# The rotation's sums of the second batch moved from VectorE to accumulating transfers that GpSimd issues

## The chip, the cores and the metric

The kernel runs on one core of a Trainium2 chip. The metric is device time in microseconds (us) of one execution; lower is better.

## The reference

Four batches of eight heads, 576 positions, head size 64. Queries and keys are rotated by position, attention is a plain softmax, and its output feeds a gated layer of 512 to 1536 to 512 features:

```python
def rotate(x):
    x1, x2 = (x[..., :half], x[..., half:])
    return np.concatenate([x1 * cos - x2 * sin, x1 * sin + x2 * cos], axis=-1)
q_rot, k_rot = (rotate(q), rotate(k))
scores = scale * np.matmul(q_rot, k_rot.transpose(0, 1, 3, 2))
attn = softmax(scores)                     # maximum subtracted, sum + 1e-9
x = np.matmul(attn, v)                     # heads side by side: 2304 x 512
out = (1 / (1 + np.exp(-(x @ w_gate))) * (x @ w_val)) @ w_out
```

The inputs are float32, and large enough (q, k and w_gate are scaled up) that the kernel carries most operands as two float16 terms. w_gate, w_val and w_out come in as 64-bit words that the kernel decodes on the chip.

## The kernel before, in words

**Tiling.** Heads go in pairs, two heads of 64 rows to the 128 partitions, so a batch has four pairs p = 0 to 3 (`NP`). For each pair the rotation needs `x`, which holds key and query side by side (128 x 2 x 576 float32, 576 KB), and `y`, the same with the halves of each head swapped (the tile `sw`, also 576 KB). With m = 0 for the keys and m = 1 for the queries, three operations each give `x = x*cos + y*sin`: the product of `x` (L416), the product of `y` (L418) and the sum (L420).

**Where the tiles lie.** Batches 0 and 1 keep `x` in `qk0[p]`, which is a piece of the tile `stk`, and TensorE takes their scores from it in float32 (L470). Batches 2 and 3 use two other buffers, `qk`, and go on into float16 terms (L482). The buffers of `sw` are two for all batches, in turn: pair p = 2 of batch 1 gets the one that p = 0 had, p = 3 the one of p = 1, and the first two pairs of batch 2 follow in the same way. A reload of `sw` (L412) therefore waits for the last operation that reads the old contents, which is the sum.

**Engines.** The rotation is done by VectorE for batches 0 and 1 and by GpSimd for batches 2 and 3. All transfers are issued by SyncE, in one queue and in one order: loads of `x` (L411) and `sw` (L412), of v (L379), of the words of w_out (L348), a copy between partition halves (L534, shown as p<-p), and the transposes of the attention weights (L537, shown as pt<-p), on which the product of weights and v waits (L547). A transfer whose semaphore isn't there yet holds all that is behind it in that queue.

**Order.** All operations are given to a planner (`Plan`) with a rank, a cost and the tiles that they read and write; it plays them through once and fixes the order of every engine and of the transfer queue. Costs are in us; `land=(a, b)` makes a task a transfer that holds one common bus for a and is complete b later. VectorE and GpSimd share a `port` in this model. Only the order comes out of it, with the waits that the data need.

**Stages.** The first 200 us decode w_gate, w_val and w_out on VectorE and ScalarE (L295, L298, L302, L354) while batch 0's attention runs. The last third of w_out's decoding, the end of batch 0's attention and the rotation of batch 1 meet between 160 and 230 us of the span. Then comes the hidden layer of batch 0's second half (L598), the first long run of matmuls, whose scale needs a maximum over partitions (`allmax`, L252, L254 on VectorE, L257).

Of the kernel before, what the change touches and what calls it, by code (L numbers as in the profile page):

```python
# [16 lines left out]
ALU = mybir.AluOpType  # L17
# [17 lines left out]
class Plan:  # L35
# [27 lines left out]
    def order(self):  # L63
        N = len(self.tasks)
        succ = [[] for _ in range(N)]
        left = [len(p) for p in self.preds]
        for n, p in enumerate(self.preds):
            for m in p:
                succ[m].append(n)
        free, wait, ready, done = {}, {}, {}, [None] * N  # L70

        def offer(n):
            for e, _ in self.tasks[n][0]:
                t = 0.0
                for m in self.preds[n]:
                    e0, end, land = done[m]
                    t = max(t, end if e0 == e and not land else end + land + self.HOP)
                heapq.heappush(wait.setdefault(e, []), (t, self.tasks[n][1], n))
                ready.setdefault(e, [])
                free.setdefault(e, 0.0)  # L80

        for n in range(N):
            if not left[n]:
                offer(n)
        starts, bus, port = [], 0.0, 0.0
        while len(starts) < N:
            best = None
            for e in free:
                w, r = wait[e], ready[e]
                while w and done[w[0][2]]:  # L90
                    heapq.heappop(w)
                while r and done[r[0][1]]:
                    heapq.heappop(r)
                if r or w:
                    t = free[e] if r else max(free[e], w[0][0])
                    if best is None or t < best[0]:
                        best = (t, e)
            t, e = best
            w, r = wait[e], ready[e]
            while w and w[0][0] <= t:  # L100
                _, rank, n = heapq.heappop(w)
                if not done[n]:
                    heapq.heappush(r, (rank, n))

            held = e in ("DVE", "POOL") and port > t + 0.2
            fit = [x for x in r if not held or (e == "DVE" and not self.tasks[x[1]][4])]
            if fit:
                x = min(fit)
                r.remove(x)
                heapq.heapify(r)  # L110
            else:
                x = heapq.heappop(r)
            n = x[1]
            where, rank, fn, land, locks = self.tasks[n]
            cost = dict(where)[e]
            if e == "POOL" or (e == "DVE" and locks):
                t = max(t, port)
                port = t + cost
            if land:

                bus = max(bus, t + cost) + land[0]
                done[n] = (e, t + cost, bus + land[1] - t - cost)
            else:
                done[n] = (e, t + cost, 0.0)
            free[e] = t + cost
            starts.append((t, n, e))
            for m in succ[n]:
                left[m] -= 1
                if not left[m]:
                    offer(m)  # L130
        self.done = done
        return sorted(starts)
# [7 lines left out]
def c_dve(n, psum=False, two=False):  # L140
    return 0.07 + n / 960 + (0.08 if psum else 0) + (0.1 if two else 0)


def c_act(n):
    return 0.24 + n * 0.0009


def c_pool(n, two=False):
    return 0.16 + n * (0.0025 if two else 0.0011)
# [7 lines left out]
def rope_attention_then_sigmoid_glu(ctx: ExitStack, tc: tile.TileContext, qk, v, w_in, w_out, tables, out):  # L157
    nc = tc.nc
    V, A, G, T, Y = nc.vector, nc.scalar, nc.gpsimd, nc.tensor, nc.sync
# [48 lines left out]
    P = Plan()  # L208
    turn = {}

    def ring(name, n):
        k = turn[name] = (turn.get(name, -1) + 1) % n
        return k

    def op(e, us, rank, reads, writes, fn, port=False):
        P.add(((e, us),), rank, reads, writes, lambda _: fn(eng.get(e)), port=port)
# [4 lines left out]
    def either(places, rank, reads, writes, fn, port=True):  # L221
        P.add(tuple(places), rank, reads, writes, lambda e: fn(eng[e]), port=port)

    def dma(rank, reads, writes, kb, fn, also=()):
        P.add((("SP", 0.45),), rank, reads, writes, lambda _: fn(), land=(kb / 280, 1.6), also=also)
# [7 lines left out]
    def tiny(rank, reads, writes, fn, us=0.2):  # L233
        op("DVE", us, rank, reads, writes, lambda E: fn())
# [26 lines left out]
    def allsum(rank, src, n, where, reads):  # L261

        ps, Z = where
        mm(0.4, rank, reads + ["zero"], [Z], lambda: T.matmul(ps[:, 0:n], lhsT=ones, rhs=src, start=True, stop=True))
        return ps[:, 0:n]
# [3 lines left out]
    def m_place():  # L269
        m = ring("m", 3)  # L270
        return m_ps[m], ("m", m)
# [127 lines left out]
    def keys_queries(b, p, rank):  # L399

        z = ring("sw", 2)
        Z = [("sw", z, m) for m in range(2)]
        if b < NW:
            x, X = qk0[p], [("stk", n) for n in range(8 * p, 8 * p + 8)]
            X = [X[0:4], X[4:8]]
        else:
            r = ring("qk", 2)
            x, X = qkr[r], [[("qk", r, m)] for m in range(2)]
        y = sw[z]
        early = -8.5 if b == p == 0 else rank - 0.1  # L410
        dma(early, [], X[0] + X[1], 576, lambda: Y.dma_start(out=x, in_=qk[b, p, 0]))  # L411
        dma(early, [], Z, 576, lambda: Y.dma_start(out=y, in_=qk[b, p, 1]))  # L412
        gate = ["tab"] + ([("ws", 8 + p)] if b == 1 else [])
        places = [("POOL", c_pool(S, two=True))] if b > 1 else [("DVE", c_dve(S, two=True))]
        for m in range(2):
            either(places, rank, gate, X[m], lambda E, m=m: E.tensor_tensor(  # L416
                out=x[:, m], in0=x[:, m], in1=tab[:, 0], op=ALU.mult))
            either(places, rank, gate, [Z[m]], lambda E, m=m: E.tensor_tensor(  # L418
                out=y[:, m], in0=y[:, m], in1=tab[:, 1], op=ALU.mult))
            either(places, rank, [Z[m]], X[m], lambda E, m=m: E.tensor_tensor(  # L420
                out=x[:, m], in0=x[:, m], in1=y[:, m], op=ALU.add))
        if b < NW:
            slots[b, p] = p, None, -1.0 / D ** 0.5
            return
        X = X[0] + X[1]
        t, k = ring("stk", 3), ring("q_m", 4)
        M = ("q_m", k)
        e16 = y.rearrange("p m c -> p (m c)").bitcast(F16).rearrange("p (n c) -> p n c", n=4)
        for m in range(2):
            op("ACT", c_act(S) + 0.2, rank, [X[m]], ["sink", M], lambda E, m=m: A.activation(  # L430
                sink, x[:, m], AF.Abs, accum_out=q_m[:, k, m:m + 1]))
        top = allsum(rank, q_m[:, k], 2, m_place(), [M])
        Q = ("q_s", k)
        place = ("m", turn["m"])
        pow2(rank, top, q_s[:, k], q_i[:, k], 14, [place], [Q])
        n = 4 * (b - NW) + p
        se = q_e[:, n:n + 1]
        tiny(rank, [Q], [("q_e", n)], lambda: V.scalar_tensor_tensor(
            out=se, in0=q_i[:, k, 0:1], scalar=-1.0 / D ** 0.5, in1=q_i[:, k, 1:2], op0=ALU.mult, op1=ALU.mult))
        for m, hi, lo in ((0, 1, 2), (1, 0, 3)):  # L440
            op("ACT", c_act(S), rank, [X[m], Q], Z, lambda E, m=m, hi=hi: scaled(A, e16[:, hi], x[:, m], q_s[:, k, m:m + 1]))
            op2(c_dve(S, two=True), rank, [X[m], Q], Z, lambda E, m=m, hi=hi, lo=lo: rest(
                e16[:, lo], x[:, m], q_s[:, k, m:m + 1], e16[:, hi]))
        W = [("stk", n) for n in range(12 * t, 12 * t + 12)]
        for h in range(2):
            U = W[6 * h:6 * h + 6]
            hs = slice(64 * h, 64 * h + 64)
            dst = stk[:, t, h]
            dma(rank, Z, U[0:2], 216, lambda hs=hs, dst=dst: Y.dma_start(
                out=dst[0:64], in_=e16[hs, 0:3]), U)  # L450
            dma(rank, Z, U[2:3], 72, lambda hs=hs, dst=dst: Y.dma_start(
                out=dst[64:128, 0], in_=e16[hs, 3]), U)
            dma(rank, Z, U[3:4], 72, lambda hs=hs, dst=dst: Y.dma_start(
                out=dst[64:128, 1], in_=e16[hs, 2]), U)
            dma(rank, Z, U[4:6], 72, lambda hs=hs, dst=dst: Y.dma_start(
                out=dst[64:128, 2], in_=e16[hs, 1]), U)
        slots[b, p] = t, se, se
# [307 lines left out]
```

## Time and profile before

| | us |
|---|---|
| three runs, median | 740.73 |
| three runs, lowest and highest | 736.84, 741.0 |
| the profiled execution's own time | 738.06 |
| its span, first to last instruction | 736.2 |
| VectorE busy | 525.1 (71%) |
| TensorE busy | 632.9 (86%) |
| GpSimd busy | 74.9 (10%) |

Busy shares are means over the whole span. Positions in the span are in us from its first instruction. In the views, PE is TensorE, DVE VectorE, ACT ScalarE, POOL GpSimd and SP SyncE; an L with a number is the line of the kernel that issued the instruction, where helpers such as L281 (the second float16 term) stand for all that call them. "Idle before" is the time in which the engine had nothing to do, with what ended it.

### The profile page before, as it was taken

The numbers are of one execution on the slowest core, as the hardware profiler recorded it, in microseconds if no ns is written. First come the engines' busy times: TensorE is split into PE (matmuls) and PEld (weight loads), VectorE is DVE, ScalarE is ACT, GpSimd is POOL, SyncE is SP. The second block draws the span as 40 slices with busy tenths as digits, with TensorE's granted clock in tenths as the row PEclk, the third lists the DMA queues.
The fourth block names the chain that finished last, engine by engine and source line by source line (L and its number), as shares of the span: only waits on it lengthen the run. The fifth ranks groups of instructions, "written<-read, shape, count | busy, mean of one in ns | idle before, by whom it ended". The sixth has DMA issues, their size and how long they took to land.

```text
span 736.2 us, 12433 instructions
## 1 busy us (share of the span) xinstructions
PE 632.9 (86%) x4642; PEld 414.9 (56%) x4642; DVE 525.1 (71%) x1194; ACT 461.7 (63%) x940; POOL 74.9 (10%) x54
## 2 busy tenths in 40 slices
PE   2366885773199999999999899999999999999997
PEld 1134563451066644677556665587567756866753
DVE  6998899989978963787589987669968655321310
ACT  3767899876557983776666877667567655322320
POOL 0400000000033000014313022130500000000000
PEclk9999797896589999999999999999999999999999
DMA  9965744747924283387775596755774516000001
GB/s 365 316 153 133 233 154 151 195 120 203 246 83 129 52 189 93 94 187 163 160 186 134 108 202 179 165 125 119 178 152 100 131 37 151 1 1 29 1 7 37
DMA packets 187484, 100.55 MB, mean 137 GB/s; under 512 B 171040, under 2 KB 176288, under 8 KB 185376
## 3 DMA queue, kind: packets, MB, share of 16 engines
q1 hardware_dynamic: 187424, 99.77, 53.4%
q8 instruction: 36, 0.59, 0.3%
q14 instruction: 24, 0.20, 0.1%
HBM read 43.12 MB, written 4.72 MB: 65 GB/s over the span
## 4 chain that ended last, share of the span: by engine, by line
PE 69%; DVE 21%; DMA 5%; issue 3%; ACT 2%; SPq 0%; DVEq 0%; ACTq 0%
PE m L598 31%; PE m L632 19%; PE pv L547 8%; PE s L470 5%; PE s L482 4%; DVE p L281 4%; DMA pt<-p 4%; DVE p L505 3%; DVE wo L298 2%; DVE wo L302 2%; DVE w L281 1%; DVE stk L420 1%; DVE gt L281 1%; DVE sw L418 1%; DMA sw<-in_qk_dram 1%
## 5 line engine op out<-in xcount | busy, mean ns | idle before, releaser
L598 PE MATMUL m<-xt,w 128*128 128x320 f16 (+1 forms) x2304 | 302.2, 290 | 7.7 <-DVE th L608 3.5
L598 PEld LDWEIGHTS <-w 128*128 128x128 f16 x2304 | 224.6, 99 | 78.3 <-issue 14.6
L632 PE MATMUL m<-wo,gt 128*128 128x512 f16 x648 | 145.5, 379 | 1.6 <-DVE th L608 1.6
L510 ACT ACTIVATE p<-p,st 128x576 f32<-128x576 f32 x144 | 110.5, 768 | 55.5 <-DVE p L505 47.9
L281 DVE SCALAR_TENSOR_TENSOR p<-p,st,p 128x576 f16<-128x576 f32 x144 | 120.8, 868 | 21.0 <-ACT p L275 20.3
L470 PE MATMUL s<-stk 64*128 64x288 f32 (+1 forms) x320 | 70.8, 514 | 51.6 <-DVE p L505 37.2
L275 ACT ACTIVATE p<-p,st 128x576 f16<-128x576 f32 x144 | 104.4, 765 | 15.6 <-DMA pt<-p 6.4
L632 PEld LDWEIGHTS <-gt 128*128 128x128 f16 x648 | 62.4, 98 | 75.0 <-issue 5.8
L547 PE MATMUL pv<-pt,v 128*64 128x256 f16 (+3 forms) x960 | 77.2, 311 | 21.4 <-DMA pt<-p 21.4
L608 DVE SCALAR_TENSOR_TENSOR th<-th,m 128x256 f32<-128x256 f32 (+1 forms) x96 | 42.9, 450 | 68.0 <-PE m L598 65.3
L275 ACT ACTIVATE gt<-th,c_s 128x256 f16<-128x256 f32 (+1 forms) x96 | 50.3, 529 | 52.6 <-DVE th L608 51.9
L547 PEld LDWEIGHTS <-v 128*64 128x64 f16 (+1 forms) x960 | 54.6, 118 | 44.1 <-issue 30.0
L470 PEld LDWEIGHTS s<-stk 64*128 64x128 f32 (+1 forms) x320 | 35.6, 211 | 76.3 <-DVE p L505 46.8
L604 ACT ACTIVATE th<-m,gsc 128x256 f32<-128x256 f32 (+1 forms) x96 | 47.5, 494 | 41.1 <-PE m L598 40.9
L281 DVE SCALAR_TENSOR_TENSOR gt<-th,c_s,gt 128x256 f16<-128x256 f32 (+1 forms) x96 | 51.6, 542 | 18.5 <-ACT gt L275 18.3
L505 DVE TENSOR_SCALAR_CACHE_REDUCE p<-s 128x576 f32<-128x576 f32 x72 | 53.4, 750 | 15.1 <-PE s L470 14.6
L505 DVE TENSOR_SCALAR_CACHE_REDUCE p<-s,q_e 128x576 f32<-128x576 f32 x72 | 57.0, 811 | 9.8 <-PE s L482 9.3
L418 POOL TENSOR_TENSOR sw<-sw,tab 128x576 f32<-128x576 f32 x16 | 24.1, 1504 | 253.4 <-DMA sw<-in_qk_dram 222.9
L482 PE MATMUL s<-stk 128*128 128x288 f16 (+1 forms) x320 | 44.4, 287 | 3.1 <-DVE p L505 3.0
L416 POOL TENSOR_TENSOR qk<-qk,tab 128x576 f32<-128x576 f32 x16 | 25.3, 1607 | 201.7 <-DMA qk<-in_qk_dram 179.1
L482 PEld LDWEIGHTS <-stk 128*128 128x128 f16 (+1 forms) x320 | 27.5, 100 | 16.7 <-issue 8.2
L275 ACT ACTIVATE o<-m,o_s 128x512 f32<-128x512 f32 x16 | 10.9, 684 | 37.2 <-PE m L632 37.0
(94 smaller groups left out, 506.9 us busy)
## 6 DMA issues: line engine op xcount, KB each, us to landing
wo<-in_w_dram SPq DMA_DIRECT2D x12, 1024.0 KB, 5.6
sw<-in_qk_dram SPq DMA_DIRECT2D x16, 576.0 KB, 5.0
xt<-in_wo_dram SPq DMA_DIRECT2D x12, 512.0 KB, 4.7
stk<-in_qk_dram SPq DMA_DIRECT2D x8, 576.0 KB, 4.6
xt<-in_v_dram SPq DMA_DIRECT2D x4, 1152.0 KB, 7.1
qk<-in_qk_dram SPq DMA_DIRECT2D x8, 576.0 KB, 5.8
out_dram<-o SPq DMA_DIRECT2D x16, 256.0 KB, 2.0
stk<-sw SPq DMA_DIRECT2D x16, 216.0 KB, 3.5
```

Of the source, the lines that this page charges most:

```text
L275: A.activation(o, src, AF.Copy, scale=scale)
L281: V.scalar_tensor_tensor(out=o, in0=src, scalar=scale, in1=hi, op0=ALU.mult, op1=ALU.subtract)
L418: either(places, rank, gate, [Z[m]], lambda E, m=m: E.tensor_tensor(out=y[:, m], in0=y[:, m], in1=tab[:, 1], op=ALU.mult))
L470: T.matmul(s_ps[to[e]][hs if width == 64 else slice(0, 128), c, 0:288], lhsT=qT[hs, rows:rows + width], rhs=kT[hs, c * 288:c * 288 + 288], ...
L482: T.matmul(o[:, c, 0:288], lhsT=q[:, rows:rows + width], rhs=kk[:, c * 288:c * 288 + 288], start=(m == 0), stop=(m == 1))
L505: lambda E, h=h, c=c: V.tensor_scalar(out=p32[prs[c]].rearrange("p (c n) -> p c n", c=2), in0=s_ps[h][:, :, 0:288], scalar1=down, scalar2= ...
L510: lambda E, c=c: A.activation(p32[prs[c]], p32[prs[c]], AF.Exp, bias=st[:, k, 0, c:c + 1], scale=-1.0, accum_out=st[:, k, 1, c:c + 1]))
L547: T.matmul(v_ps[64 * e:64 * e + 64, 0:n], lhsT=v16[hs, p, a, g, :], rhs=pt[z][hs, c * 9 + g, 0:n], start=(first and m == 0), stop=(last an ...
L598: T.matmul(m_ps[m][:, 0:n], lhsT=w16[:, f, g, a, cc, :], rhs=x[:, cc, c, c0:c0 + n], start=(k == 0), stop=(k == 11))
L604: op("ACT", c_act(n), rank - 0.05, [("m", m), ("gsc", b, f)], [("th", r)], lambda E, m=m: A.activation(t, m_ps[m][:, 0:n], AF.Tanh, scale= ...
L608: op("DVE", c_dve(n, psum=True), rank - 0.05, [("m", m)], [("th", r)], lambda E, m=m: V.scalar_tensor_tensor(out=t, in0=t, scalar=1.0, in1 ...
L632: T.matmul(m_ps[m], lhsT=gt[:, f, a, c0:c0 + 128], rhs=wo16[:, f, c, :], start=(f == 0 and k == 0), stop=(f == NF - 1 and k == 2))
```

## The change: what it does

For batch 1 the two sums of each pair (L420, on VectorE) are left out. In their place stands one transfer per pair, issued by GpSimd, which adds all of `y` (both halves) onto `x` in SBUF. It reads `y` and the four products' results, and writes both halves of `x`. The planner gives it 1.0 us of GpSimd, 576/140 us of the bus and 2.5 us to landing, and it doesn't take the port.

```diff
             cost = dict(where)[e]
-            if e == "POOL" or (e == "DVE" and locks):
+            if (e == "POOL" and not land) or (e == "DVE" and locks):
                 t = max(t, port)
                 port = t + cost
...
             either(places, rank, gate, [Z[m]], lambda E, m=m: E.tensor_tensor(
                 out=y[:, m], in0=y[:, m], in1=tab[:, 1], op=ALU.mult))
-            either(places, rank, [Z[m]], X[m], lambda E, m=m: E.tensor_tensor(
-                out=x[:, m], in0=x[:, m], in1=y[:, m], op=ALU.add))
+            if b != 1:
+                either(places, rank, [Z[m]], X[m], lambda E, m=m: E.tensor_tensor(
+                    out=x[:, m], in0=x[:, m], in1=y[:, m], op=ALU.add))
+        if b == 1:
+
+            P.add((("POOL", 1.0),), rank, Z, X[0] + X[1], lambda _: G.dma_start(
+                out=x, in_=y, accum_op=ALU.add), land=(576 / 140, 2.5))
```

## Rows read from the trace of the kernel before

**Rows 1.** The page's first part: busy time, share of the span and instructions of each engine.

```profile
PE 632.9 (86%) x4642; PEld 414.9 (56%) x4642; DVE 525.1 (71%) x1194; ACT 461.7 (63%) x940; POOL 74.9 (10%) x54
```

**Rows 2.** Busy time by stretches of the span: stretch, its length, busy us (instructions) of the engines, the granted TensorE clock as a share of full speed, the mean share of the 16 DMA engines, GB/s.

```profile
160.00:187.00 27.00, 10.94 (x88) 6.29 (x86) 24.42 (x56) 19.40 (x42) 0.00 (x0) 0.73 0.72 187
187.00:203.00 16.00, 2.75 (x13) 1.69 (x15) 15.09 (x25) 6.43 (x13) 0.00 (x0) 0.50 0.99 261
203.00:214.00 11.00, 9.29 (x66) 5.84 (x63) 9.28 (x18) 6.17 (x14) 4.73 (x3) 0.84 0.35 126
...
370.00:430.00 60.00, 55.11 (x461) 38.02 (x460) 54.11 (x130) 44.77 (x93) 9.93 (x7) 1.00 0.71 153
...
214.00:736.00 522.00, 509.81 (x3878) 335.24 (x3875) 334.98 (x811) 306.69 (x627) 62.20 (x42) 1.00 0.48 110
```

**Rows 3.** All sums of VectorE (batches 0 and 1, eight each): duration in ns, minimum, median and maximum, first and last start. Then the busy time of L420 alone between 174 and 214 us, VectorE's and GpSimd's.

```profile
L420 DVE TENSOR_TENSOR stk<-stk,sw x16: 748/757/759, 8.7 to 226.6; 128x576 f32<-128x576 f32 x16
...
174.00:214.00 40.00, 4.53 (x6) 1.73 (x1) 0.64 0.71 202
```

**Rows 4.** VectorE in order of time around batch 1's rotation: start, us, line, operation, tiles.

```profile
174.02 0.75 DVE L420 TENSOR_TENSOR stk<-stk,sw 128x576 f32<-128x576 f32 x1
...
177.95 0.75 DVE L505 TENSOR_SCALAR_CACHE_REDUCE p<-s 128x576 f32<-128x576 f32 x1
...
179.23 0.75 DVE L418 TENSOR_TENSOR sw<-sw,tab 128x576 f32<-128x576 f32 x1
...
186.12 0.75 DVE L420 TENSOR_TENSOR stk<-stk,sw 128x576 f32<-128x576 f32 x1
...
194.82 0.76 DVE L420 TENSOR_TENSOR stk<-stk,sw 128x576 f32<-128x576 f32 x1
...
202.94 0.75 DVE L420 TENSOR_TENSOR stk<-stk,sw 128x576 f32<-128x576 f32 x1
...
226.57 0.76 DVE L420 TENSOR_TENSOR stk<-stk,sw 128x576 f32<-128x576 f32 x1
```

**Rows 5.** TensorE in order of time at the end of batch 0's attention.

```profile
178.76 2.19 PE L470 MATMUL s<-stk 64*64 64x288 f32 x8 [9.79 <-DVE p L505]
180.88 3.20 PE L547 MATMUL pv<-pt,v 128*64 128x320 f16 x30
186.92 2.29 PE L470 MATMUL s<-stk 64*128 64x288 f32 x8 [2.85 <-DVE stk L420]
202.46 4.28 PE L547 MATMUL pv<-pt,v 128*64 128x320 f16 x30 [13.25 <-DMA pt<-p]
...
213.41 0.38 PE L257 MATMUL pv<-row,ones 1*128 1x1 f32 x2 [1.71 <-DVE row L254]
213.72 9.95 PE L598 MATMUL m<-xt,w 128*128 128x320 f16 x72
```

**Rows 6.** SyncE's queue in order of time: start and length of the issue, line, transfer. The first line is of another transpose, for comparison.

```profile
168.80 3.55 SPq L537 DMA_TRANSPOSE pt<-p  x1
...
184.11 1.99 SPq L537 DMA_TRANSPOSE pt<-p  x1
186.20 0.52 SPq L348 DMA_DIRECT2D xt<-in_wo_dram  x1
186.90 0.33 SPq L412 DMA_DIRECT2D sw<-in_qk_dram  x1
187.28 5.67 SPq L537 DMA_TRANSPOSE pt<-p  x1
...
193.68 0.62 SPq L534 DMA_DIRECT2D p<-p  x1
...
195.60 0.33 SPq L412 DMA_DIRECT2D sw<-in_qk_dram  x1
198.51 1.83 SPq L537 DMA_TRANSPOSE pt<-p  x1
...
203.72 0.33 SPq L412 DMA_DIRECT2D sw<-in_qk_dram  x1
221.68 0.33 SPq L379 DMA_DIRECT2D xt<-in_v_dram  x1
```

**Rows 7.** VectorE and GpSimd where both work at once, in order of time for each; then the same decoding line (L302) and GpSimd's first products (L416) over the whole span, ns minimum, median, maximum.

```profile
209.50 1.78 DVE L302 SCALAR_TENSOR_TENSOR wo<-wo,xt 128x512 f32<-128x512 f32 x1
211.21 1.95 DVE L418 TENSOR_TENSOR sw<-sw,tab 128x576 f32<-128x576 f32 x1
213.08 0.27 DVE L254 TENSOR_REDUCE row<-pv 1x1 f32<-1x128 f32 x1
...
209.19 1.55 POOL L418 TENSOR_TENSOR sw<-sw,tab 128x576 f32<-128x576 f32 x1 [173.75 <-DMA sw<-in_qk_dram]
...
L302 DVE SCALAR_TENSOR_TENSOR wo<-wo,xt x10: 672/691/1783, 161.8 to 209.5; 128x512 f32<-128x512 f32 x10
...
L416 POOL TENSOR_TENSOR qk<-qk,tab x16: 1400/1414/2394, 28.0 to 518.0; 128x576 f32<-128x576 f32 x16
```

**Rows 8.** From issue to landing of the loads of `sw`, in us, minimum, median and maximum: of the three between 186 and 216 us, then of all sixteen.

```profile
DMA to landing us min/median/max: 5.3/5.7/6.0
...
DMA to landing us min/median/max: 3.7/5.0/14.2
```

## The prediction

> **What bounds the kernel now.** I read the page's busy shares first. TensorE leads with 632.9 us and GpSimd has almost nothing to do [rows 1], so sums taken from VectorE matter only where VectorE, and not TensorE, sets the pace. The table by stretches shows where that is. From 160 to 187 us VectorE is busy 24.42 of 27 us and TensorE 10.94; from 187 to 203 us TensorE has 2.75 us of work in 16; from 214 us to the end it is busy 509.81 of 522 us [rows 2]. So TensorE is full from about 214 us on, and what the change is worth is how much earlier that long run of matmuls starts, as long as the work behind it stays fed.
>
> Then the order of time in that stage. Up to 187 us the chain goes through VectorE. Its minimum over scores at 177.95 frees the score buffer for the matmuls at 178.76, these go before the product at 180.88 [rows 4, 5], and behind that come the last attention weights and the transposes that SyncE issues at 184.11 and 187.28 [rows 6]. From 187 to 202 us the chain is transfers: the transpose at 187.28 takes 5.67 us to issue, the copy p<-p goes at 193.68, the last transpose at 198.51 [rows 6], TensorE waits 13.25 us for it [rows 5], and the DMA engines are at 0.99 [rows 2]. The third piece is VectorE again: the maximum over partitions at 213.08 stands behind a decoding step and a product, and TensorE waits 1.71 us for it [rows 5, 7].
>
> **The change part by part.** Out go eight sums, a median 757 ns each: 6.06 us of VectorE, six of them between 174 and 214 us [rows 3]. In come four transfers on GpSimd. What moves is every reload of `sw` behind them, which now waits for a landing in place of a VectorE instruction.
>
> *Sums on the chain.* Before 187 us only the one at 174.02 stands ahead of work on the chain; the one at 186.12 comes after the weights that the transpose at 187.28 takes [rows 4, 6]. That is -0.75 us, with 0 as the other end should the planner put something else there. The next four, up to 202.94, lie beside the transfers on which TensorE waits [rows 2, 4, 5], so they are costed at nothing; without that cover they would give another 4 x 0.76 = 3.0 us. The last two, to 226.57 [rows 4], lie beside a TensorE that is full [rows 2]: nothing, and at most 1.5 us.
>
> *The transfer itself.* No accumulating transfer is in this trace. The nearest row is the load of the same 576 KB: 5.3 to 6.0 us here, 3.7 to 14.2 over the span [rows 8]. An accumulate must read `x` as well as `y`; at this stretch's 261 GB/s [rows 2] another 590 KB takes 2.3 us. To GpSimd's issue I give 1.0 us, between SyncE's 0.33 for a load [rows 6] and 1.4 us, one GpSimd product [rows 7]. So from the last product to landing I take 5.7 + 2.3 + 1.0 = 9.0 us; the ends are 3.7 + 0.3 = 4.0 and 14.2 + 2.3 + 1.4 = 17.9.
>
> *The reload of `sw` and the queue.* The last product of pair 0 ends at 179.98 [rows 4], less 0.75, so its sum lands at 188.2. The reload of that buffer went at 186.90, directly ahead of the transpose at 187.28 [rows 6]: kept there, SyncE would stand 1.3 us with the transpose behind it. For pair 1 the products end at about 194.8 less two or three sums, some 193; the sum lands at 202, and the reload that went at 195.60 [rows 6] would hold the last transpose by 6 us. The planner however books 1.0 + 4.1 + 2.5 = 7.6 us, so it moves both reloads back by about that, and only the excess, 9.0 - 7.6 = 1.4 us, can hold the queue, if a transpose is next behind. The reloads for batch 2 (203.72 and later) stand ahead of a load that goes at 221.68 [rows 6]; a landing up to 15 us later is hidden there.
>
> *The transposes.* With the reload gone from before it, the transpose at 187.28 may issue faster: 5.67 us here, 1.99 for the one at 184.11, 3.55 for the one at 168.80 [rows 6]. A load of 512 KB (186.20) is still ahead of it, so I take 3.55: -2.1 us. Pair 1's accumulate takes the place of a reload in engines that are already full, with one more read: +2.3 us on p<-p and the last transpose. Net +0.2; the ends are -3.7 (1.99, no collision) and +4.6 (two extra reads, nothing gained).
>
> *The third piece.* The decoding step at 209.50 took 1.78 us where its median is 0.69, and the product behind it 1.95 where the same product took 0.75 at 179.23, while GpSimd worked on batch 2's first pair [rows 4, 7]: 2.3 us together. GpSimd started at 209.19 because that pair's `sw` was asked for at 203.72 [rows 6, 7]. With pair 2's sum landing some 8 us after the products instead of 0.75, GpSimd starts some 7 us later, past 213, and the collision falls on work beside a full TensorE. TensorE can gain only its wait there: -1.7 us, other end 0.
>
> *Sum.* -0.75 + 0.2 - 1.7 = -2.3 us. On the profiled execution's 738.06 (its span is 736.2) that gives 735.8. The median of the runs, 740.73, lies 2.7 us above that execution, so a median would be 738.4. After 214 us I change nothing: TensorE's idle time there is 12.2 us, 4.9 of it between 370 and 430 [rows 2], and a new order may double or remove the latter.
>
> **The rivals.**
>
> *Slower: a late sum holds SyncE.* The mechanism is one wait: the reload of `sw` stands in the one transfer queue, and the transposes on the chain stand behind it. It decides from about 9 us, where the transfer begins to take more than the planner's 7.6. For it: the engines are full just then [rows 2], a same-sized load has taken 14.2 us [rows 8], and VectorE is busy nine tenths of the time [rows 2] and the two engines hinder each other: VectorE's steps beside GpSimd ran over 1 us long, and GpSimd's products, 1.41 us in the median, took up to 2.39 [rows 7]; an issue by GpSimd may be stretched in the same way. Against it: DMA has room around 180 to 187 us, when pair 0's goes (0.72 over the stretch), and some reloads may be planned past the last transpose. At 12 us, two holds of 4.4 less the gains of 2.5 make +6.3, or 747; at 14.2, +10.7, or 751.
>
> The Trainium skill (SBUF — State Buffer, "SBUF: two separate sides") has a rule that speaks against this change: VectorE's two-port operations keep GpSimd from writing a transfer's descriptors, and a transfer of about 620 ns then takes about 3100. No row here has a transfer issued by GpSimd to test it on. By that page each sum would land 2.5 us later still, an estimate: 11.5 us in place of 9.0, two holds of 3.9 less 2.5, +5.3, or 746.
>
> *Faster by more: the queue opens.* The transpose at 187.28 falls to 1.99 us with no collision, and the other terms hold: -0.75 - 3.7 - 1.7 = -6.2; half of the idle time after 370 us goes too, -2.5. That gives 729.4 on the profiled execution, 732 as a median. For it: the 5.67 us stand directly behind two loads, and 13 us of TensorE's wait hang on them. Against: the reload must go somewhere, and the engines stay full.
>
> *Nothing comes of it.* 6.06 us of 525.1 [rows 1, 3] are off the chain for the most part, and a planner that re-deals the orders of all engines gives back in later stalls what it gained: 740.7, within the 4.9 us of [rows 2].
>
> **How the numbers follow.** Forecast 0.45, slower 0.24, faster 0.16, nothing 0.15. What a measurement of this kernel can tell from no change is about 1%, 7.4 us: below 733.3 or above 748.1. Of the faster rival I put 0.12 below 733.3, and 0.02 from the others; of the slower one 0.14 above 748.1, and 0.04 from forecast and nothing. That leaves 0.68 within 1%. The forecast's own range by its ends is -6.2 to +4.6 us, 734.5 to 745.3 as a median. For 8 in 10 it must reach into both rivals: 732 to 749.
>
> **What would show it.** Right: eight sums fewer on VectorE; GpSimd with four transfers landing 8 to 10 us after the last product; the transpose of batch 0's last full tile issued in under 4 us; GpSimd's first product of batch 2 after the maximum over partitions, and that maximum without a wait of over 0.5 us on TensorE; TensorE's long run starting at 211 to 212 us in place of 213.7. Wrong: SyncE idle ahead of a reload of `sw` with a transpose behind it; VectorE idle ahead of a product of pair 2 or 3 for want of `sw`; landings over 12 us; or a start of the long run at 212 with an end no earlier, which would put the loss in the orders after 214 us.

## The result, and the profile after

Four runs of the changed kernel took 744.41 to 752.74 us, median 748.32; the kernel before took 738.79 on the same chip. The ratio is 1.0122, 95% interval 1.0081 to 1.0163: about 9 us lost where 2.3 were forecast as gained. The profiled execution took 745.35 us (span 743.6); of the other three runs one was faster (744.41) and two were slower (751.29, 752.74). In all ratios a run that took over 1.5% longer than the fastest of its kernel counts as slow and is left out, which concerns two of the ten runs of e14. Lines from the sum on have moved: the sum itself is L421, the new transfer L425, later lines are 5 higher.

Busy shares of the changed kernel, its GpSimd transfer queue, and the windows of [rows 2]:

```profile
PE 640.7 (86%) x4642; PEld 417.6 (56%) x4642; DVE 523.1 (70%) x1186; ACT 463.6 (62%) x940; POOL 79.1 (11%) x58
...
q0 software_dynamic: 576, 2.36, 1.8%
...
160.00:187.00 27.00, 10.58 (x70) 6.32 (x70) 22.95 (x54) 18.46 (x40) 1.00 (x1) 0.69 0.85 193
187.00:203.00 16.00, 8.03 (x46) 4.46 (x44) 13.96 (x27) 7.87 (x18) 1.73 (x2) 0.61 0.95 240
203.00:214.00 11.00, 4.87 (x16) 2.33 (x16) 8.84 (x19) 7.51 (x16) 0.73 (x2) 0.50 1.08 325
...
214.00:260.00 46.00, 43.24 (x314) 28.85 (x311) 37.89 (x77) 32.10 (x66) 12.65 (x9) 0.92 0.39 94
```

VectorE has its eight sums fewer, and 160 to 187 us shows it (24.42 to 22.95 us). Its whole busy time fell by 2.0 us only, though, and not by the sums' 6.06: other steps of it grew longer beside GpSimd, as shown further down. The loss is in 203 to 214 us: TensorE has 4.87 us of work there instead of 9.29, and the DMA engines, at 0.35 in [rows 2], are full. TensorE is granted half its full clock there (the level of 1.2 GHz) and 0.92 on average from 214 to 260 us, where [rows 2] have 1.00 from 214 us on.

The same stage in order of time: SyncE's queue, with two lines on what it waited for (us in total, times, longest; stk<-sw are the sums' transfers), then GpSimd's transfers with the summary of their landings, then TensorE. A landing is counted from the start of the issue.

```profile
171.74 3.76 SPq L542 DMA_TRANSPOSE pt<-p  x1
...
186.56 0.33 SPq L412 DMA_DIRECT2D sw<-in_qk_dram  x1
...
192.12 4.38 SPq L542 DMA_TRANSPOSE pt<-p  x1
196.60 0.52 SPq L348 DMA_DIRECT2D xt<-in_wo_dram  x1
197.17 4.50 SPq L542 DMA_TRANSPOSE pt<-p  x1
201.77 0.79 SPq L539 DMA_DIRECT2D p<-p  x1
...
207.13 6.19 SPq L542 DMA_TRANSPOSE pt<-p  x2
...
SPq L412 <- DMA stk<-sw: 12.0, 3, 8.1
SPq L542 <- PE pv L552: 4.7, 1, 4.7
...
178.94 1.00 POOL L425 DMA_DIRECT2D stk<-sw  x1 [143.24 <-DVE wo L295]
190.88 0.87 POOL L425 DMA_DIRECT2D stk<-sw  x1 [10.93 <-DMA sw<-in_qk_dram]
197.34 0.86 POOL L425 DMA_DIRECT2D stk<-sw  x1 [5.60 <-DVE sw L418]
...
DMA to landing us min/median/max: 5.5/8.2/9.3
...
181.68 2.19 PE L475 MATMUL s<-stk 64*64 64x288 f32 x8 [8.74 <-DVE p L510]
186.59 2.29 PE L475 MATMUL s<-stk 64*128 64x288 f32 x8 [2.73 <-DMA stk<-sw]
188.81 3.27 PE L552 MATMUL pv<-pt,v 128*64 128x320 f16 x30
...
213.39 4.35 PE L552 MATMUL pv<-pt,v 128*64 128x320 f16 x30 [1.52 <-DMA pt<-p]
```

Count from the transpose at 171.74 (168.80 in [rows 6]). What lies ahead of it ran 2.9 us later, which says little: in e5 and e12, which keep the old order there, this transpose lies at 169.08 and at 173.03 us. The last product of batch 0 comes 41.65 us behind it, 33.66 before: 8.0 us lost. They arise in two places.

First, the scores of batch 1's pair 0 (186.59) now stand ahead of the product (188.81) and wait 2.73 us for the accumulating transfer; in [rows 5] the product came first, and the scores at 186.92 held nothing up. So the product begins 17.07 us behind the transpose and not 12.08, 5.0 us later. The next transpose comes later by as much, since it overwrites what the product reads: SyncE waits 4.7 us for the product and issues at 192.12, when it ends; before, the product of 180.88 ended at 184.08 and the transpose went at 184.11.

Second, the transposes: from the one at 192.12 to the last product 21.27 us pass. From its twin at 184.11 it was 18.35, so 2.9 us are lost here. The one at 192.12, 1.2 us behind a transfer of GpSimd's, takes 4.38 us to issue, where its twin took 1.99 [rows 6]; the one at 197.17 is joined by a transfer after 0.17 us and lands in 9.3 us (7.8 before); the last, at 207.13, lands in 6.2 us (3.9 before).

Behind the last product the changed kernel needs 530.2 us to the end of its span, the kernel before 533.7, so 3.5 of the 8.0 us come back there. This execution thus shows a loss of 4.5 us from the transpose on. The loss of 9 us in the median is twice that, and the two slowest runs have no trace, so about half of it is seen in no row of the changed kernel.

### The profile page after: what moved, and what is told of

It is laid out like the page before. It is cut to its first block, busy times and chain, and to the rows that moved or that the text cites. A ratio compares the mean times of both kernels' runs of the same rounds, so it can differ in the third digit from the quotient of the medians.

```text
span 743.6 us, 12440 instructions
## 1 busy us (share of the span) xinstructions
PE 640.7 (86%) x4642; PEld 417.6 (56%) x4642; DVE 523.1 (70%) x1186; ACT 463.6 (62%) x940; POOL 79.1 (11%) x58
## 4 chain that ended last, share of the span: by engine, by line
PE 72%; DVE 15%; DMA 6%; ACT 3%; issue 3%; SPq 1%; DVEq 0%; ACTq 0%; POOLq 0%
PE m L603 34%; PE m L637 18%; PE pv L552 9%; PE s L475 5%; PE s L487 4%; DMA pt<-p 3%; DVE p L281 3%; DVE p L510 2%; DVE wo L298 1%; DVE w L281 1%; DMA stk<-sw 1%; DVE wo L302 1%; DVE sw L418 1%; DMA sw<-in_qk_dram 1%; DMA p<-p 1%
## 5 line engine op out<-in xcount | busy, mean ns | idle before, releaser
L281 DVE SCALAR_TENSOR_TENSOR p<-p,st,p 128x576 f16<-128x576 f32 x144 | 119.4, 858 | 25.1 <-ACT p L275 24.6
L475 PE MATMUL s<-stk 64*128 64x288 f32 (+1 forms) x320 | 76.6, 540 | 65.3 <-DVE p L510 50.4
L475 PEld LDWEIGHTS s<-stk 64*128 64x128 f32 (+1 forms) x320 | 38.5, 224 | 92.9 <-DVE p L510 62.4
L281 DVE SCALAR_TENSOR_TENSOR gt<-th,c_s,gt 128x256 f16<-128x256 f32 (+1 forms) x96 | 54.8, 575 | 20.5 <-ACT gt L275 20.4
L416 POOL TENSOR_TENSOR qk<-qk,tab 128x576 f32<-128x576 f32 x16 | 25.7, 1629 | 208.2 <-DMA qk<-in_qk_dram 109.4
L275 ACT ACTIVATE xt<-pv 128x256 f16<-128x256 f32 (+1 forms) x32 | 13.0, 406 | 34.3 <-PE pv L552 34.3
```

The costliest lines, as they stand in the source:

```text
L275: A.activation(o, src, AF.Copy, scale=scale)
L281: V.scalar_tensor_tensor(out=o, in0=src, scalar=scale, in1=hi, op0=ALU.mult, op1=ALU.subtract)
L475: T.matmul(s_ps[to[e]][hs if width == 64 else slice(0, 128), c, 0:288], lhsT=qT[hs, rows:rows + width], rhs=kT[hs, c * 288:c * 288 + 288], ...
```

## The experiments

All ratios are to the kernel before, run on the same chip at the same time. "Last product" is the product at 202.46 in [rows 5], counted as above from the transpose that is at 168.80 in [rows 6]; 33.66 us before.

**Was there a gain to be had?** e14 takes batch 1's sums away from the kernel before and puts nothing in their place.

```diff
-            either(places, rank, [Z[m]], X[m], lambda E, m=m: E.tensor_tensor(
+            either(places, rank, [Z[m]], X[m], lambda E, m=m: b == 1 or E.tensor_tensor(
                 out=x[:, m], in0=x[:, m], in1=y[:, m], op=ALU.add))
```

> The kernel before with batch 1's eight sums left out of its orders and nothing in their place: what the relief of VectorE could give at best, with no transfer and no new order. By the prediction's term for the sums: -0.75 us, with the six before 214 us uncovered at most -4.5, and -1.7 if the collision on VectorE goes with them, so 734 to 740, ratio 0.994 to 1.000. Theory that the relief is worth nothing because transfers set the pace from 187 to 203 us: ratio 0.998 to 1.001. Below 0.993 would mean that the change gave up a real gain.

Measured 0.9981 [0.9941, 1.002]. In the old orders even sums that cost nothing give no gain that can be measured. The interval, -4.4 to +1.5 us, still has room for the forecast's 2.3. The trace fits transfers that set the pace: the last product comes 32.79 us behind its transpose, 0.9 us earlier than with the sums. e8 moves the sums to ordinary GpSimd additions, planned anew, with no transfer:

```diff
-            either(places, rank, [Z[m]], X[m], lambda E, m=m: E.tensor_tensor(
+            either([("POOL", c_pool(S, two=True))] if b else places, rank, [Z[m]], X[m], lambda E, m=m: E.tensor_tensor(
                 out=x[:, m], in0=x[:, m], in1=y[:, m], op=ALU.add))
```

> The kernel before with batch 1's eight sums as ordinary additions on GpSimd (about 1.5 us each), planned anew; VectorE gets the same relief, with no transfer and no landing to wait for. Theory O: the plan keeps batch 0's products ahead of pair 0's scores, and the relief of VectorE shows: 0 to 3 us faster than before, 736 to 740 us. If any new order costs: slower by 3 us and more.

1.0004 [0.9977, 1.0031]: the same relief of VectorE, the same time as before, though each sum takes 1720 ns on GpSimd in the mean. So taking the sums from VectorE need not cost anything; the 9 us come with the transfers and the orders that were planned for them.

**The new orders.** e2 keeps the changed kernel's orders and puts one VectorE sum of 1.3 us where each transfer was.

```diff
-            P.add((("POOL", 1.0),), rank, Z, X[0] + X[1], lambda _: G.dma_start(
-                out=x, in_=y, accum_op=ALU.add), land=(576 / 140, 2.5))
+            P.add((("POOL", 1.0),), rank, Z, X[0] + X[1], lambda _: V.tensor_tensor(
+                out=x, in0=x, in1=y, op=ALU.add), land=(576 / 140, 2.5))
```

> The order of the changed kernel, but at the transfer's place VectorE does one sum of both halves (four of them, about 1.3 us each); no accumulating transfer is left. Theory T: without the transfers the time falls back to that of the kernel before, within 3 us. Theory O: the scores of pair 0 still stand ahead of batch 0's third product, but wait for 1.3 us and not for 8, so about half of the loss is left, 3 to 6 us over the kernel before. If the rest of the re-dealt order is what costs, it stays at 7 to 10 us over.

1.0118 [1.0075, 1.0161], as much as the change. I read this as orders that cost by themselves, and e6, which also puts pair 0's scores back behind the product, seemed to agree:

```diff
+        s = next(x for x in self.starts if x[1] == self.score)
+        self.starts.remove(s)
+        self.starts.insert(1 + next(k for k, x in enumerate(self.starts) if x[1] == self.product), s)
...
```

> Run e2 (the changed kernel's order, sums by VectorE, no transfer) with pair 0's first scores moved behind batch 0's third product, as in e3. Theory O: 3 to 5 us faster than e2, so 743 to 746 us; what is then left over the kernel before, some 4 us, is the rest of the new order, the same as in e3, and the transfers cost nothing. Theory T: falls to the kernel before, and the 4 us that e3 kept are the transfers' own.

1.0105 [1.0058, 1.0151]. That reading fell with e13, the same orders without any sum:

```diff
-            P.add((("POOL", 1.0),), rank, Z, X[0] + X[1], lambda _: G.dma_start(
-                out=x, in_=y, accum_op=ALU.add), land=(576 / 140, 2.5))
+            P.add((("POOL", 1.0),), rank, Z, X[0] + X[1], lambda _: None, land=(576 / 140, 2.5))
```

> The changed kernel's orders with nothing in the place of the four accumulating transfers: batch 1's rotation is left without its sums, so neither VectorE nor a transfer pays for them. Theory that the re-dealt orders cost by themselves: 745 to 750, ratio 1.008 to 1.014, the last product of batch 0 begins 7 us or more later, counted from the same transposes at about 164 us, than in the kernel before. Rival, that in this order the loss comes from the sums (from the transfers in the changed kernel, from 1.3 us each of VectorE in e2_new_order_vector_sums): 737 to 742, ratio 0.996 to 1.003.

1.0017 [0.9988, 1.0046]. TensorE of e13:

```profile
179.17 5.34 PE L474 MATMUL s<-stk 64*64 64x288 f32 x16 [8.73 <-DVE p L509]
184.44 4.16 PE L551 MATMUL pv<-pt,v 128*64 128x320 f16 x30
194.05 1.32 PE L474 MATMUL s<-stk 64*128 64x288 f32 x2 [5.46 <-DVE p L509]
197.20 3.61 PE L474 MATMUL s<-stk 64*128 64x288 f32 x8 [1.82 <-DVE p L509]
...
207.54 2.92 PE L551 MATMUL pv<-pt,v 128*64 128x320 f16 x30 [0.18 <-DMA pt<-p]
```

The last product is 38.32 us behind its transpose (169.22), still 4.7 later than before, and yet the time is that of before: in between TensorE does scores of batch 1 that it would do later anyway. An order alone costs nothing here; a sum placed in it does, on VectorE as much as in a transfer. Why 1.3 us of VectorE, four times, cost e2 as much as the transfers was not tried further. e2's trace shows only where it loses ahead of the last product, 3.3 us against e13: the sums at 177.37, 190.75 and 197.15 us stand on VectorE ahead of the weights that the copy p<-p takes, and that copy goes 29.90 us behind the transpose, 26.67 in e13. In e6 it is 29.89, so the product that begins 3.2 us earlier than in e2 (13.13 us behind the transpose, not 16.30) brings the last product no nearer (41.63, 41.59 in e2).

**Waiting or traffic?** e15 is e13 with a transfer back in each place, which adds 384 KB of `x` onto a scratch tile that nobody reads.

```diff
             P.add((("POOL", 1.0),), rank, Z, X[0] + X[1], lambda _: G.dma_start(
-                out=x, in_=y, accum_op=ALU.add), land=(576 / 140, 2.5))
+                out=idle, in_=x.rearrange("p m c -> p (m c)")[:, 0:768], accum_op=ALU.add), land=(576 / 140, 2.5))
```

> As e13_new_order_no_sums (the changed kernel's orders without batch 1's sums), with a transfer back at each of the four places, which adds 384 KB of the products onto a scratch tile that nobody reads: traffic in the changed kernel's order, and no wait on it. Theory that the changed kernel loses by waiting for its sums: 739 to 743, ratio 0.999 to 1.005. Rival, that it loses by what the transfers take from the transposes beside them: 745 to 750, ratio 1.008 to 1.014, with transposes that land in 8 us or more. Between them, 1.005 to 1.008, both have a part.

1.0063 [1.0023, 1.0103]. By these figures both have a part: traffic of two thirds of the bytes 1.0063 - 1.0017, some 3.4 us; the waits and the remaining third 1.0122 - 1.0063, some 4.4. The intervals overlap, and each of the two is known to about 4 us only. The traces, one execution each, give a split as well. TensorE of e15, whose first transpose is at 170.08, then all four in us: how far the product ahead of the last one (180.88 in [rows 5]) begins behind the transpose that is at 168.80 in [rows 6], and the time from the transpose that waits for this product (184.11 in [rows 6]) to the last product.

```profile
185.29 3.94 PE L553 MATMUL pv<-pt,v 128*64 128x320 f16 x30
...
210.23 4.35 PE L553 MATMUL pv<-pt,v 128*64 128x320 f16 x30 [2.25 <-DMA pt<-p]
```

| | product, behind the transpose | from the waiting transpose to the last product |
|---|---|---|
| kernel before | 12.08 | 18.35 |
| e13, new order, no sums | 15.22 | 18.91 |
| e15, with traffic | 15.21 | 20.97 |
| changed kernel | 17.07 | 21.27 |

The order moves the product by 3.1 us, which e13 makes up behind the last product (530.3 us from there to the end of its span, 533.7 in the kernel before). The wait for the sum adds 1.9 us, and the transfers add 2.1 to 2.4 us between the transposes and the last product. Does mending the order give the wait's part back? e3 is the change with pair 0's scores behind the product on TensorE and all else alike (the three lines of e6):

> The changed kernel with one thing moved: on TensorE the first scores of batch 1's pair 0 stand behind batch 0's third product and not ahead of it. Theory O: that product starts some 5 us earlier in its stretch, and the time falls by 3 to 5 us against the changed kernel, to 743 to 746 us. Theory T: it changes nothing beyond 1 us, since the transposes behind it are late for the traffic.

1.0065 [1.0028, 1.0101]: by the time over half a per cent back, though the intervals overlap. The trace doesn't show that gain. In its execution (747.05 us, where the six runs took 740.00 to 747.48) the product no longer waits for the sum, but it comes 18.12 us behind the transpose, later than in the changed kernel, and the last product 46.65:

```profile
176.15 2.11 SPq L547 DMA_TRANSPOSE pt<-p  x1
...
176.49 1.00 POOL L428 DMA_DIRECT2D stk<-sw  x1 [141.25 <-DVE wo L298]
...
187.40 4.35 PE L557 MATMUL pv<-pt,v 128*64 128x320 f16 x30 [5.99 <-DMA pt<-p]
```

Pair 0's transfer started 0.34 us behind the transpose that this product needs, and they landed in 10.7 and 11.1 us; in the changed kernel's own trace the same two, 0.40 us apart, took 7.6 and 5.3. So a transfer beside a transpose can cost much more in one execution than in another, and what mending the order is worth stays open. e4 changes the plan in another way and tells it that the transfer takes nothing of the bus:

```diff
-                out=x, in_=y, accum_op=ALU.add), land=(576 / 140, 2.5))
+                out=x, in_=y, accum_op=ALU.add), land=(0.01, 6.6))
```

> The changed kernel, but the planner books the transfer with no time on the common bus (0.01 and 6.6 us to landing in place of 4.1 and 2.5), so it doesn't push batch 0's transposes back in its model; the program does the same work. Theory O: the plan puts batch 0's products ahead of pair 0's scores again, and the time is that of the kernel before or up to 3 us under it. Theory T: as slow as the changed kernel, 745 to 752 us.

1.0126 [1.0076, 1.0176]: the product went ahead of pair 0's scores again, but the second full transpose, issued at 190.43, now met a transfer at 194.53 and landed in 10.7 us.

**Holding SyncE.** e1 takes the kernel before, in its orders, with the transfer in the place of the second sum.

```diff
+    def add_up(E, b, x, y, m):
+        if b != 1:
+            E.tensor_tensor(out=x[:, m], in0=x[:, m], in1=y[:, m], op=ALU.add)
+        elif m == 1:
+            G.dma_start(out=x, in_=y, accum_op=ALU.add)
...
```

> The order of every engine as the kernel before had it; at the place of a pair's second sum GpSimd issues the accumulating transfer, the first sum is dropped. Theory O (the new order): the loss sits in TensorE's new order, where the scores of batch 1's pair 0 stand ahead of batch 0's third product and wait for the sum to land; with the old order that is gone, and the time is within 1% of the kernel before, 735 to 746 us. Theory T (the transfer itself): the transfers take room from the transposes, and SyncE stands at the reloads of sw, which here keep their old places ahead of transposes; slower than before by 6 to 12 us, and SyncE waits at the second reload until about 203 us.

1.0204 [1.0155, 1.0254]. SyncE, GpSimd and TensorE of e1:

```profile
199.78 0.54 SPq L348 DMA_DIRECT2D xt<-in_wo_dram  x1
208.42 0.33 SPq L418 DMA_DIRECT2D sw<-in_qk_dram  x1
208.80 2.45 SPq L542 DMA_TRANSPOSE pt<-p  x1
...
199.99 0.86 POOL L403 DMA_DIRECT2D stk<-sw  x1 [15.75 <-DVE sw L424]
...
215.58 4.35 PE L552 MATMUL pv<-pt,v 128*64 128x320 f16 x30 [22.12 <-DMA pt<-p]
```

This is the hold of the slower rival, as described: the reload at 208.42 waits 8 us for the transfer of 199.99, and the last transpose stands behind it. e7 is e1 with the reloads of pairs 2 and 3 moved behind the second and the last transpose:

```diff
+        for late, first in ((self.reload[1, 2], self.turned[3]), (self.reload[1, 3], self.turned[4])):
+            s = next(x for x in self.starts if x[1] == late)
+            self.starts.remove(s)
+            self.starts.insert(1 + next(k for k, x in enumerate(self.starts) if x[1] == first), s)
...
```

> Run e1 (the old order, sums by accumulating transfers) with two entries of the transfer queue moved: the reload of sw for pair 2 behind the second of batch 0's last three transposes, that for pair 3 behind the third. If e1 was slow for SyncE standing 8 us at the reload of pair 3: 10 to 15 us faster than e1, 739 to 744 us. If it was slow for the traffic: as e1, over 750 us.

1.0183 [1.0137, 1.023]. The hold is gone, the last product is 5 us nearer to its transpose (38.61 us, 43.93 in e1), and the time is nearly the same. So the hold is real but was not what cost most. Much of what e7 loses lies behind its last product: in the 60 us from there TensorE is idle for 8.3 us, 2.3 in the kernel before, and its granted clock is 0.80, 0.89 and 0.94 in the first 15, the next 15 and the last 30 of them, where it was 0.86, 1.00 and 1.00. Among the waits are 2.89 us for the maximum at 224.15 and 2.78 us for VectorE at 258.85. What in the change of e7 sets them off was not tried.

**What a transfer does to a transpose.** e5 leaves the kernel before as it is, its sums on VectorE too, and adds traffic: behind each pair's second sum GpSimd adds 384 KB onto a scratch tile.

```diff
+    def add_up(E, b, x, y, m):
+        E.tensor_tensor(out=x[:, m], in0=x[:, m], in1=y[:, m], op=ALU.add)
+        if b == 1 and m == 1:
+            G.dma_start(out=idle, in_=x.rearrange("p m c -> p (m c)")[:, 0:768], accum_op=ALU.add)
...
```

> The kernel before, with its order and all sums on VectorE; behind each pair's second sum of batch 1 GpSimd also issues an accumulating transfer of 384 KB (x onto a scratch tile), for which nobody waits. So it adds the traffic of two thirds of the change's transfers and nothing else. If traffic beside batch 0's transposes costs (theory T): 2 to 4 us slower than before, with transposes that land in 8 to 11 us. If order and waits alone cost (theory O): within 1.5 us of before.

1.019 [1.0153, 1.0228], with nobody waiting for it. The next four take it apart: e9 keeps pair 0's transfer alone, e10 makes that one a plain copy, e11 keeps pair 1's (`p == 1`), e12 those of pairs 2 and 3 (`p >= 2`). In the cut below the first two lines are e9 against e5, the last two e10 against e9.

```diff
-        if b == 1 and m == 1:
+        if b == 1 and p == 0 and m == 1:
...
-            G.dma_start(out=idle, in_=x.rearrange("p m c -> p (m c)")[:, 0:768], accum_op=ALU.add)
+            G.dma_start(out=idle, in_=x.rearrange("p m c -> p (m c)")[:, 0:768])
```

> Of the three transfers of e5_traffic_alone that lie before 230 us only pair 0's is kept: 384 KB of its sums are added onto a scratch tile that nobody reads, issued by GpSimd behind the sum, while batch 0's second transpose is being issued. Order, sums and result are those of the kernel before. Theory of the jam (a transfer that starts beside a transpose holds both up): the transpose and the transfer land some 18 us after their issue again, the last product begins near 213 us, and the time is 749 to 755, ratio 1.014 to 1.020. Theory of shared bandwidth (each transfer costs its own bytes): the last product begins 2 to 4 us late, 741 to 744, ratio 1.003 to 1.006.

> As e9_transfer_of_pair_0, but GpSimd's transfer copies the same 384 KB onto the scratch tile and adds nothing. If the addition inside the transfer is what jams, the second transpose lands in 8 to 10 us and the time is 739 to 743, ratio 0.999 to 1.005. If any transfer of GpSimd's queue beside a transpose jams it, it lands in 15 to 18 us and the time is as in e9_transfer_of_pair_0, ratio 1.014 to 1.020.

> As e5_traffic_alone, but only pair 1's transfer of 384 KB is kept, which GpSimd issues at about 196 us, beside the copy p<-p and ahead of the last transpose of batch 0. Theory of the jam: no transpose is being issued when it starts, so p<-p lands 1 to 3 us later, the last product begins by 206 us, and the time is 739 to 743, ratio 1.000 to 1.005. Theory that any such transfer in this stage is dear: the last transpose goes at 203 us or later, last product from 208 us, ratio 1.010 or more.

> As e5_traffic_alone, but only the transfers of pairs 2 and 3 are kept, 384 KB each, issued behind batch 0's last transpose (about 204 and 228 us), where TensorE is full or about to be. Both theories: the last product begins at 202 to 204 us and the time is that of the kernel before, ratio 0.997 to 1.003. A ratio of 1.008 or more would mean that a transfer costs also where no transpose of the chain is near, by what it takes from the loads of the MLP's weights or from SyncE's queue.

| | ratio | last product, us |
|---|---|---|
| e9, pair 0 | 1.01 [1.0051, 1.015] | 43.80 |
| e10, pair 0, plain copy | 1.0071 [1.0035, 1.0106] | 40.98 |
| e11, pair 1 | 1.0062 [1.0035, 1.0089] | 36.97 |
| e12, pairs 2 and 3 | 1.0015 [0.9989, 1.0042] | 34.71 |

The cost is where the transfer lies: behind the last transpose none can be measured, beside the transposes 384 KB cost 5 to 7 us. The excesses of e9, e11 and e12 add up to 0.0177, e5 has 0.019; that proves little, since in e5 the jam held pair 1's transfer back to 206.39 us, where it is not the case of e11. The jam's mechanism is as expected in e9, its price by the time smaller (747.15, not 749 to 755); e11's lies between the figures of the two theories. The addition is not needed for it: with the plain copy the transpose landed in 15.8 us and the copy in 14.8, and its interval overlaps that of e9, though the time too is under what was expected. In e9 the second full transpose and the transfer start together; SyncE, GpSimd, then TensorE, and the landings from issue in the stretch (the last column, us):

```profile
189.93 5.60 SPq L542 DMA_TRANSPOSE pt<-p  x1
...
196.25 0.62 SPq L539 DMA_DIRECT2D p<-p  x1
...
210.40 1.32 SPq L542 DMA_TRANSPOSE pt<-p  x1
...
190.08 1.00 POOL L403 DMA_DIRECT2D idle<-stk  x1 [154.50 <-DVE wo L296]
...
214.27 3.72 PE L552 MATMUL pv<-pt,v 128*64 128x320 f16 x30 [22.64 <-DMA pt<-p]
...
xt<-in_wo_dram SPq DMA_DIRECT2D x2, 512.0 KB, 14.2
idle<-stk POOLq DMA_DIRECT2D x1, 384.0 KB, 18.0
p<-p SPq DMA_DIRECT2D x1, 144.0 KB, 14.1
pt<-p SPq DMA_TRANSPOSE x1, 18.3
```

Without the transfer that transpose landed in 7.8 us and p<-p in 4.8 (the kernel before). One microsecond inside the jam, 198 to 199 us of e9, then one of the changed kernel with its transpose of 197.17 in flight (201 to 202 us):

```profile
DMA packets 74, 0.03 MB, mean 33 GB/s; under 512 B 69, under 2 KB 69, under 8 KB 74
...
q1 hardware_dynamic: 69, 0.02, 114.9%
q0 software_dynamic: 5, 0.02, 10.4%
```

```profile
DMA packets 837, 0.21 MB, mean 214 GB/s; under 512 B 837, under 2 KB 837, under 8 KB 837
...
q1 hardware_dynamic: 837, 0.21, 106.0%
```

In the first, packets of GpSimd's queue (q0) come in between the small packets of a transpose (q1): the engines show as busy and pass 74 packets in a microsecond. In the second, with none of GpSimd's among them, they pass 837. That the mixing is what slows them is inferred from such stretches and was not tried by itself. The profiled execution of the changed kernel mostly escaped this: the transfer issued at 197.34 moved its first bytes behind 202.75 us, when the transpose's packets were nearly through. What decides whether they mix isn't known.

## Why the prediction was wrong

*What bounds the kernel*: right, and e14 agrees: from 187 to 202 us transfers set the pace. The prediction should have drawn the other half of that reading: engines at 0.99 are where added transfers cost.

*Sums on the chain, -0.75*: not refuted. In e14's trace the last product comes 0.9 us earlier, and its time, -1.4 us (1 - 0.9981 of 740), holds the term within an interval of -4.4 to +1.5.

*The transfer itself, 9.0 us*: right. The issues took 0.86 to 1.00 us and the landings, the issue included, 5.5 to 9.3; from the end of a pair's last product to the landing it was 6.1 to 9.8 us, 8.8 in the median. But the time from the products to the landing decides only for whoever waits; the price was elsewhere.

*The reload and the queue*: a little over what was allowed, and it cost the last product nothing. SyncE stood 2.3 us for pair 0's landing, up to 186.56, where 1.4 were allowed, with no transpose next behind. It stood 1.6 us for pair 2's, up to 206.66, with the last transpose next behind; but that had to wait for the copy p<-p, which landed at 207.1. The longest hold, 8.1 us up to 222.12 for pair 3's landing, stood ahead of a load at 225.13 and no transpose of batch 0, where the prediction had said that a late landing is hidden.

*Net +0.2 for the transposes*: this step failed. I priced the collision by bytes, "with one more read: +2.3 us", and set a gain of 2.1 against it. From the first of the three transposes to the last product the changed kernel took 2.9 us more (21.27, 18.35 before). The price by bytes is near what the transfers added in its profiled execution (2.4 us, against e13), so there it was the gain that failed: the transpose at 187.28 became that of 197.17, issued in 4.50 us and not 5.67, but it landed 1.5 us later, and the one ahead of it went from 1.99 to 4.38. Even with no transfer at all there is none in this stretch: 18.91 us in e13. And bytes are no upper bound. Beside transposes 384 KB cost 4.6 us in e11 and 7.4 in e9, where by bytes they come to 1.5 us, or 3.0 with a second read, at 261 GB/s.

*"The planner moves both reloads back" and nothing else moves*: this failed too. The planner, with the transfer's 4.1 us on its one bus, dealt pair 0's scores ahead of batch 0's product, and so put a wait for the late sum at the head of TensorE's queue. I looked for the wait in SyncE's queue and not in the queue of the sum's own reader, and the prediction has nothing on the transpose at 184.11, which waits for that product. The path through the product was priced at nothing. In the trace the product came 5.0 us later: 3.1 by the order, which is made up later, and 1.9 by the wait. By the time, mending that place gave back 4.2 us (e3 against the change), but e3's trace doesn't show it.

*The third piece, -1.7*: the wait went, but the collision only moved. TensorE no longer waits at the maximum. GpSimd started at 213.83, ahead of the maximum at 221.61 and not behind it as forecast, and met three decoding steps instead. Its second pair, from 225.96, met the steps of VectorE that stand directly ahead of a scale that TensorE needs:

```profile
213.59 2.27 DVE L295 TENSOR_SCALAR wo<-xt 128x512 int32<-128x512 int32 x1
...
228.22 1.36 DVE L358 TENSOR_TENSOR wo_s<-wo_b,w_i 128x12 f32<-128x12 f32 x1
229.50 1.75 DVE L281 SCALAR_TENSOR_TENSOR gt<-th,c_s,gt 128x320 f16<-128x320 f32 x1
231.18 0.15 DVE L360 TENSOR_REDUCE wo_m<-wo_s 128x1 f32<-128x12 f32 x1
...
225.96 1.72 POOL L418 TENSOR_TENSOR sw<-sw,tab 128x576 f32<-128x576 f32 x1 [5.56 <-DMA sw<-in_qk_dram]
...
231.39 0.38 PE L264 MATMUL m<-wo_m,ones 128*128 128x1 f32 x2 [2.76 <-DVE wo_m L360]
```

The first took 2.27 us, five times its usual 0.42. L358 took 1.36 us where it took 0.17 in the kernel before, the L281 behind it 1.75 where it is 0.55, and TensorE waited 2.76 us for the result of L360 (0.20 before). The 84 matmuls behind that wait took 13.24 us, with a granted clock of 0.87 in the mean, where the same 84 took 11.58 at 1.00.

*The rivals*: the outcome lies between the slower rival's 747 and 751 and inside the range of 732 to 749, but not by its mechanism: no hold of SyncE made the last product late, and e7 shows that taking even e1's long hold away wins little. The second "slower" figure, 746, is no better: the Trainium skill (SBUF — State Buffer, "SBUF: two separate sides") lets VectorE's two-port operations keep GpSimd from writing descriptors. Here the issues beside a VectorE busy 87% of 187 to 203 us took 0.86 and 0.87 us, and the transfers landed in the time worked out without that rule; but no row says which of VectorE's operations there are two-port ones, so the rule itself isn't tested. "Nothing comes of it" was right about the relief (e8, e14) and wrong in taking the transfer and the new orders as free.

## What to carry to other kernels

Before work is moved into transfers, look at the DMA engines' share in the very stretch where they will run, and at what else is in them: beside transposes that the critical path waits for, a transfer nobody waits for cost 5 to 7 us, and behind them nothing that could be measured. Follow a late result first to its reader's queue, where other work stands behind it. And take the work away altogether in one run (as e14 does): if that gains nothing clear of the noise, a new place for it has little to win.

## What the runs showed that I had not expected

- A transfer from GpSimd's queue that starts 0.15 to 0.19 us behind a full transpose can hold both for 15 to 18 us (e9 18.0 and 18.3, e10 14.8 and 15.8, e5 17.5 and 18.0); everything that SyncE issued in the next 10 us landed in 10 to 15 us. In the changed kernel the same start gave 9.3 for both, and in e3 a start 0.34 us behind gave 10.7 and 11.1.
- The share of the DMA engines is no measure of what they move: 187 to 203 us of e9 has 1.12 at 154 GB/s, the kernel before 0.99 at 261 [rows 2].
- A later last product need not cost anything: e13's is 4.7 us late at the same total, since TensorE filled the time with scores.
